# Maxima over partitions by TensorE and VectorE in place of GpSimd, in an attention and feed-forward kernel

## The chip, the cores and the metric

The kernel runs on one core of one Trainium2 chip. The core has five engines with a queue each: TensorE (PE in the profile: matmuls, with a part PEld for the loads of weights), VectorE (DVE), ScalarE (ACT), GpSimd (POOL) and SyncE (SP), which here issues DMAs. Each takes its instructions in order and waits at semaphores for the others. The metric is device time in microseconds (us) of one launch, less is better. Between runs of one kernel some 0.2% lie.

## The reference

A kernelised linear attention, followed by a feed-forward layer without a residual. For each of 8 batches and 8 heads, with 576 positions of 64 numbers:

```python
def phi(x):                                   # x is q or k, scaled by D ** -0.25
    proj = np.einsum('bhsd,md->bhsm', x, omega)          # 128 features
    h = proj - np.sum(x * x, axis=-1, keepdims=True) / 2.0
    h = h - np.max(h, axis=-1, keepdims=True)
    return np.exp(h) / np.sqrt(m)
q_p, k_p = (phi(q_s), phi(k_s))
kv = np.einsum('bhsm,bhsd->bhmd', k_p, v)
z = np.sum(k_p, axis=2)
num = np.einsum('bhsm,bhmd->bhsd', q_p, kv)
den = np.einsum('bhsm,bhm->bhs', q_p, z)[..., None] + 1e-06
x = num / den                                 # then (4608 tokens, 512)
h = x @ w_in                                  # 2048 wide
sp = np.where(h > 20.0, h, np.log1p(np.exp(np.minimum(h, 20.0))))
out = (h * np.tanh(sp)) @ w_out
```

All inputs and outputs are float32.

## The kernel before

**Numbers in two halves.** Most products run in float16, each float32 operand being split into a high half and the rest of it (`cast` and `rest`, lines 71 to 87), and a product of two such operands is three matmuls: low by high, high by low, high by high. For that the operands are brought into float16's range by a power of two: one scale per batch for `v` (tiles `p_v`, `s_v`), one for `w_in` and one for `w_out` (`p_w`, `s_w`). Each scale is the power of two below the largest magnitude in the whole operand: a maximum along the free dimension on VectorE, then a maximum over the 128 partitions, then the exponent's bits alone (`bitwise_and` with 0x7F800000), a floor, a reciprocal and a factor. `over_partitions` (L116) is the step over partitions: one GpSimd instruction, PARTITION_ALL_REDUCE (L118), which leaves the maximum in every partition. `pow2` (L131) is the whole sequence behind it.

**The stages.** Tokens go in 36 tiles of 128 (`q_task`), batches in 4 pairs of heads each (`k_task`), and the feed-forward layer in 18 chunks of 256 tokens. For each pair of heads: features of `k` (matmuls `pk`, L364), their maximum (`mxk`, L389) and difference (`ek`, L398) on VectorE, the exponential on ScalarE (L404), the halves `kp`, and the product with `v` into `pkv` (L485), where `vb` holds the halves of `v`: ScalarE applies the scale in place (L474), VectorE casts (L76), GpSimd subtracts (L83), for one part of the tasks. For each token tile: features `pq`, the same steps to `qn`, a transposing DMA to `qp` (L521), the product with `kv` into `pn` (L535), the division (L546 to L551), the halves `xs` and a transposing DMA to `xT`. For each chunk: `ff_in` with matmuls `ph` (L733), the activation on ScalarE (`mish`, L918), the halves `g` (L85), and `ff_out` with matmuls `po` (L1060). The last three chunks use sums and differences of blocks (`ff_in7`, `ff_out7`; `p_s`, `p_a`, `q_s`, `q_a`) in place of the whole products. The first chunk and the first two batches run in float32.

**GpSimd's part.** Besides the all-reduces it makes the low halves of `q` and `k` (`sq`, `sk`), of most `x` (`xs`) and of `v` (`vb`), all by L83.

**The order.** The program is written down in slots. `agenda` holds generators, each with the slot at which it goes on; `step()` runs those that are due and advances by one slot; a `yield n` inside a task means: go on n slots later. In the long middle part one slot comes with each group of 24 `ph` matmuls or of 12 `po` matmuls. `give()` starts the next `k_task` or `q_task`; when a batch's last `k_task` starts, `v_task` of the next batch is put 16 slots later (`V1`). At build time a scheduler orders each engine's queue: an instruction that is ready goes in the order in which it was written, and `tc.high_priority(PRIO)` moves what is inside it 400 places to the front. From the order follow all semaphores.

**`v_task` (L277).** It loads the batch's four `vf` tiles (a pool of 5 buffers, freed when the halves `vb` are made), takes a maximum of each on VectorE (`vmx`, L287), and then, at high priority, the maximum of the four (`vam`, L294) and `pow2`. `w_scale` (L204) does the same for a weight; `scale_w` (L1195) calls it at high priority. PSUM tiles with the tag "a" (`pk`, `pq`, `pn`, `pkv`, the transposed tiles) share 4 buffers. `idle` (L95) is a 128x512 float16 constant that the matmuls of `spin` read at the start.

Of the kernel before, what the change touches and what calls it, by code (L numbers as in the profile page):

```python
# [10 lines left out]
F32 = mybir.dt.float32  # L11
I32 = mybir.dt.int32
# [3 lines left out]
ALU = mybir.AluOpType  # L16
AX = mybir.AxisListType
# [5 lines left out]
TOP = 2.0 ** 14  # L23
KVC = 2.0 ** -23
TX = 2.0 ** 12
# [5 lines left out]
def tile_kernel(  # L31
# [10 lines left out]
    nc = tc.nc  # L42
    P = 128
# [17 lines left out]
    const = ctx.enter_context(tc.tile_pool(name="const", bufs=1))  # L61
# [3 lines left out]
    ps_a = ctx.enter_context(tc.tile_pool(name="ps_a", bufs=4, space=PSUM))  # L65
# [3 lines left out]
    act, dve, pool = nc.scalar, nc.vector, nc.gpsimd  # L69
# [25 lines left out]
    idle = const.tile([P, 512], F16, name="idle")  # L95
# [9 lines left out]
    ident = const.tile([P, P], F32, name="ident")  # L105
# [10 lines left out]
    def over_partitions(src, tag):  # L116
        allm = const.tile([P, 1], F32, name=f"allm_{tag}")
        pool.partition_all_reduce(  # L118
            out_ap=allm, in_ap=src, channels=P, reduce_op=bass.bass_isa.ReduceOp.max
        )  # L120
        return allm

    def top_over(p, tag, top):

        dve.tensor_scalar_max(p, p, 2.0 ** -100)
        s = const.tile([P, 1], F32, name=f"s_{tag}")
        dve.reciprocal(out=s, in_=p)
        dve.tensor_scalar_mul(s, s, top)
        return p, s

    def pow2(amax, tag, top):  # L131


        allm = over_partitions(amax, tag)
        p = const.tile([P, 1], F32, name=f"p_{tag}")
        dve.tensor_scalar(
            out=p.bitcast(I32), in0=allm.bitcast(I32), scalar1=0x7F800000, scalar2=None,
            op0=ALU.bitwise_and,
        )
        return top_over(p, tag, top)  # L140
# [27 lines left out]
    @contextmanager  # L168
    def behind(nth, first=0):
        with ExitStack() as st:  # L170
            for ins in anchors.get(nth, ())[first:]:
                st.enter_context(tc.issue_after(ins))
            yield
# [30 lines left out]
    def w_scale(n, tag):  # L204

        am = const.tile([P, 1], F32, name=f"am_{tag}")
        for i in range(NB):
            must(1, "w", n, i)
        dve.tensor_reduce(out=am, in_=wmax[n], axis=AX.X, op=ALU.max)
        return pow2(am, tag, TX)  # L210

    def w_split(n, i, s):
        src = flat32(slots[w_at(n, i)])
# [22 lines left out]
    def must(n, *key):  # L236
        assert done.get(key, 0) >= n, key
# [34 lines left out]
    def fetch_v(b, hp):  # L272
        t = sb.tile([P, 10, D1], F32, tag="vf", name=f"vf{b}_{hp}", bufs=5)
        nc.sync.dma_start(out=t, in_=vL[b, hp])
        return t

    def v_task(b):  # L277
        vt = []
        for hp in range(HP):
            vt.append(loaded.pop(f"v{b}_{hp}", None) or fetch_v(b, hp))  # L280
        if b == 0:
            vstate[0] = (vt, None, None)
        yield 3 if b else 6
        mx = sb.tile([P, HP], F32, tag="vmx", name=f"vmx{b}", bufs=2)
        for hp in range(HP):
            with behind(AV if b == 0 else None, 1):
                dve.tensor_reduce(  # L287
                    out=mx[:, hp:hp + 1], in_=vt[hp][:, :, 0:D], axis=AX.XY, op=ALU.max,
                    apply_absolute_value=True,
                )  # L290
            yield 0 if hp % 2 == 0 or b == 0 else 1
        am = sb.tile([P, 1], F32, tag="vam", name=f"vam{b}")
        with tc.high_priority(PRIO):
            dve.tensor_reduce(out=am, in_=mx, axis=AX.X, op=ALU.max)  # L294
            p, s = pow2(am, f"v{b}", TOP)
        vstate[b] = (vt, p, s)

    kv = {}
# [803 lines left out]
    W_LOAD, W_GAP, PRIO = 1, 1, 400  # L1102
# [76 lines left out]
    def give():  # L1179
        if given[0] < len(items):  # L1180
            it = items[given[0]]
            given[0] += 1
            start((k_task if it[0] == "k" else q_task)(given[0] - 1, *it[1:]))
            if it[0] == "k" and it[2] == HP - 1 and it[1] + 1 < B:
                start(v_task(it[1] + 1), V1)
# [9 lines left out]
    def scale_w(n):  # L1195
        with tc.high_priority(PRIO):
            p_w[n], s_w[n] = w_scale(n, f"w{n}")
# [4 lines left out]
    for what in PREL.split():  # L1202
# [8 lines left out]
        else:  # L1211
            loaded[f"w0_{i}"] = fetch_w(0, i, nc.sync)
    start(v_task(0), V0)
    for i, when in enumerate(FIRST):
        at(when, give)
# [93 lines left out]
```

## Time and profile before

| what | us |
|---|---|
| median of 3 runs | 952.98 (951.78 to 953.53) |
| the profiled execution, its own time | 954.62 |
| its span, first to last instruction | 952.8 |
| PE busy | 922.3 |
| DVE busy | 710.1 |
| ACT busy | 658.7 |
| POOL busy | 222.2 |
| mean granted clock of TensorE | 0.989 |

The ten all-reduces are short in the view by line: 3.7 us for the eight of `v`, 0.7 us for the two of the weights. They start at 27.37 (batch 0), 58.25 (w_in), 63.33 (batch 1), 110.55 (batch 2), 111.94 (w_out), 223.07, 296.73, 407.02, 518.61 and 638.89 us (batches 3 to 7). GpSimd's first elementwise work (L83) starts at 120.23 us.

How to read it: a row of a timeline has the start in us from the span's start, the busy time in us, engine, line, operation, the tile written and the tiles read, shapes, and the number of instructions merged into it; brackets at its end give the idle time of that engine just before it, and what ended it. A row of the waits has who waited for whom, the us in total, how often, and the longest. In the view by windows a row has the stretch, the busy time of PE, PEld, DVE, ACT and POOL with their instructions, the granted clock, the share of the DMA engines and GB/s. In groups by line the numbers behind the count are busy us, mean ns of one, and the idle time before them.

### The profile page before, as it was taken

To read this page: it belongs to the slowest core of one execution; us is meant where nothing else is said; L and a number is where in the kernel's file an instruction comes from. 1 tells how busy PE (TensorE), PEld (TensorE's weight loads), DVE (VectorE), ACT (ScalarE), POOL (GpSimd) and SP (SyncE) were. 2 spreads that over 40 slices of the span, in tenths; PEclk is the share of its full clock that TensorE was granted. 3 is DMA by queue.
4 is the path that set the end of the run, shared out by engine and by line. 5 is a ranking of instruction groups with operands and counts; after the bars stand their busy time and mean duration, and the time that the engine had idled before them with its cause. 6 is when DMAs were issued, how large, how long until landed. Compare 5 with 4: busy or idle time off the path is not lost. (4 is left out here: it accounts for less than half of the span.)

```text
span 952.8 us, 21094 instructions
## 1 busy us (share of the span) xinstructions
PE 922.3 (97%) x8774; PEld 689.1 (72%) x8774; DVE 710.1 (75%) x1226; ACT 658.7 (69%) x873; POOL 222.2 (23%) x141
## 2 busy tenths in 40 slices
PE   9799989999999999998999899999999999999998
PEld 6688764676677677776777667777777776779997
DVE  4799887686678778787687886776877766658775
ACT  5668975678777787867676866678876876345442
POOL 0000041343323323323221323224322222200000
PEclk9799999999999999999999999999999999999999
DMA  9766233421731356323532246321543137973421
GB/s 297 265 222 212 96 80 85 92 82 46 145 80 51 105 117 135 83 70 96 115 85 77 76 119 120 101 70 46 129 103 97 34 79 153 218 212 100 154 70 45
DMA packets 153056, 108.69 MB, mean 114 GB/s; under 512 B 112832, under 2 KB 125248, under 8 KB 152960
## 3 DMA queue, kind: packets, MB, share of 16 engines
q1 hardware_dynamic: 152640, 106.75, 43.0%
q8 instruction: 69, 1.13, 0.5%
q10 hardware_dynamic: 320, 0.59, 0.3%
q14 instruction: 27, 0.22, 0.1%
HBM read 63.14 MB, written 17.83 MB: 85 GB/s over the span
## 5 line engine op out<-in xcount | busy, mean ns | idle before, releaser
L733 PE MATMUL ph<-xT,w 128*128 128x256 f16 (+1 forms) x2816 | 345.6, 279 | 4.4 <-ACT h L918 4.4
L1060 PE MATMUL po<-wo,g 128*128 128x512 f16 x1344 | 308.6, 379 | 0.0
L733 PEld LDWEIGHTS <-w 128*128 128x128 f16 x2688 | 262.8, 98 | 54.2 <-issue 6.0
L1060 PEld LDWEIGHTS <-g 128*128 128x128 f16 x1344 | 127.2, 98 | 132.7
L918 ACT ACTIVATE h<-ph,us 128x512 f32<-128x512 f32 (+3 forms) x152 | 83.0, 572 | 49.3 <-PE ph L733 48.4
L85 DVE SCALAR_TENSOR_TENSOR g<-h,us,g 128x1024 f16<-128x1024 f32 (+3 forms) x76 | 103.3, 1371 | 14.6 <-ACT g L74 14.4
L83 POOL TENSOR_TENSOR sq<-fq,sq 64x1024 f16<-64x1024 f32 x31 | 72.7, 2347 | 145.5 <-issue 86.3
L83 POOL TENSOR_TENSOR sk<-fk,sk 64x1152 f16<-64x1152 f32 x24 | 59.3, 2471 | 113.7 <-ACT sk L74 92.2
L83 POOL TENSOR_TENSOR xs<-x,xs 128x512 f16<-128x512 f32 (+1 forms) x35 | 42.2, 1206 | 158.9 <-DVE xs L76 108.2
L918 ACT ACT_TABLE_LOAD x56 | 71.8, 1283 | 1.0
L404 ACT ACT_TABLE_LOAD x53 | 68.0, 1283 | 4.2 <-DVE ek L398 3.3
L83 DVE TENSOR_TENSOR qn<-eq,qn 128x1024 f16<-128x1024 f32 x31 | 39.1, 1260 | 33.2 <-ACT qn L74 33.2
L869 PEld LDWEIGHTS <-w 128*128 128x128 f16 x1008 | 59.0, 98 | 2.8
L404 ACT ACTIVATE eq<-eq,lnt 128x1024 f32<-128x1024 f32 x31 | 35.6, 1149 | 36.6 <-DVE eq L398 36.4
L389 DVE TENSOR_REDUCE mxq<-pq 128x4 f32<-128x512 f32 x72 | 46.7, 680 | 16.2 <-PE pq L364 15.3
L74 ACT ACTIVATE g<-h,us 128x1024 f16<-128x1024 f32 (+3 forms) x64 | 58.2, 933 | 0.9
L389 DVE TENSOR_REDUCE mxk<-pk 128x4 f32<-128x512 f32 (+1 forms) x96 | 49.5, 547 | 11.7 <-PE pk L379 4.3
L83 DVE TENSOR_TENSOR kp<-ek,kp 128x1152 f16<-128x1152 f32 x24 | 36.7, 1529 | 22.6 <-ACT kp L74 21.8
L83 POOL TENSOR_TENSOR vb<-vf,vb 128x640 f16<-128x640 f32 x24 | 39.0, 1627 | 61.7 <-DVE vb L76 43.9
L1007 PEld LDWEIGHTS <-gb 128*128 128x128 f16 x504 | 48.3, 98 | 5.2
L404 ACT ACTIVATE ek<-ek,lnt 128x1152 f32<-128x1152 f32 x24 | 30.1, 1256 | 30.0 <-DVE ek L398 29.9
L918 ACT ACTIVATE h<-h,us 128x1024 f32<-128x1024 f32 (+2 forms) x16 | 14.7, 931 | 48.1 <-DVE h L878 48.1
(165 smaller groups left out, 1363.3 us busy)
## 6 DMA issues: line engine op xcount, KB each, us to landing
w<-ds SPq DMA_DIRECT2D x48, 256.0 KB, 3.4
vf<-in_vL_dram SPq DMA_DIRECT2D x32, 325.0 KB, 3.1
out_dram<-o SPq DMA_DIRECT2D x36, 256.0 KB, 2.3
fq<-in_qT_dram SPq DMA_DIRECT2D x31, 256.0 KB, 3.5
fk<-in_kT_dram SPq DMA_DIRECT2D x24, 256.0 KB, 3.7
raw<-in_w_out_dram SPq DMA_DIRECT2D x5, 1024.0 KB, 8.1
wo<-in_w_in_dram SPq DMA_DIRECT2D x4, 1024.0 KB, 10.6
raw<-in_w_in_dram SPq DMA_DIRECT2D x4, 1024.0 KB, 15.0
```

The source lines that it names most:

```text
L74: act.activation(out, in_, AF.Copy, scale=scale)
L83: eng.tensor_tensor(out=out, in0=in_, in1=hi, op=ALU.subtract)
L85: eng.scalar_tensor_tensor(out=out, in0=in_, scalar=scale, in1=hi, op0=ALU.mult, op1=ALU.subtract)
L389: sub = dve.tensor_reduce(out=mx[:, lo:hi], in_=pp[:, :m, :], axis=AX.X, op=ALU.max, negate=by_act)
L404: last = act.activation(e, e, AF.Exp, bias=lnt)
L733: nc.tensor.matmul(out=ph[:, i, :], lhsT=wi(a, k, f) if c else wi0(k, f), rhs=xT[c][:, y, k, :] if c else xT0()[:, k, :], start=n == 0, st ...
L869: nc.tensor.matmul(out=ph[:, i, :], lhsT=left(gr, op_l, i, a, k), rhs=x_region(c, r)[:, y, k0 + k, :], start=n == 0, stop=n == len(mm) - 1,)
L918: act.activation(h[:, :, lo:hi], ph[:, :, lo:hi], AF.Mish, scale=us[:, 0:1])
L1007: nc.tensor.matmul(out=ps, lhsT=gT[c, n][:, i, a, f, :], rhs=rhs, start=f == 0 and (a, y) == (1, 0), stop=f == FG - 1 and (a, y) == (0, 0),)
L1060: nc.tensor.matmul(out=po[i], lhsT=gT[c, gr][:, a, f % FG, i * P:(i + 1) * P], rhs=wo(y, f), start=f == 0 and (a, y) == parts[0], stop=f = ...
```

## The change

From batch 2 on, and for `w_out`, the maximum over partitions is made by `pow2_pe`. TensorE transposes the 128x1 column into one row of a PSUM tile (`row`, tag "a"), VectorE takes the maximum of that row into one element and masks its exponent, and TensorE multiplies a row of 128 ones by that element, so that it stands in all partitions of a second PSUM tile (`every`, tag "a"). The rest on VectorE is as it was. The ones are written once, into the first partition of `idle`. Batches 0 and 1, and `w_in`, stay as they were.

In `v_task`, for those batches, the maximum `vam` and what follows have no high priority any more, and there are two places at which the task pauses for a slot: after `vam`, and between VectorE's masking and the product. For `w_out` the generator is run through at once, inside the high priority of `scale_w`.

```diff
+    ones = []
+
+    def pow2_pe(amax, tag, top):
+
+        row = ps_a.tile([P, P], F32, tag="a", name=f"row_{tag}")
+        nc.tensor.transpose(out=row[0:1, :], in_=amax, identity=ident)
+        one = const.tile([P, 1], F32, name=f"one_{tag}")[0:1]
+        dve.tensor_reduce(out=one, in_=row[0:1, :], axis=AX.X, op=ALU.max)
+        dve.tensor_scalar(
+            out=one.bitcast(I32), in0=one.bitcast(I32), scalar1=0x7F800000, scalar2=None,
+            op0=ALU.bitwise_and,
+        )
+        yield 1
+        if not ones:
+            ones.append(idle.bitcast(F32)[0:1, 0:P])
+            dve.memset(ones[0], 1.0)
+        every = ps_a.tile([P, 1], F32, tag="a", name=f"every_{tag}")
+        nc.tensor.matmul(out=every, lhsT=ones[0], rhs=one, start=True, stop=True)
+        p = const.tile([P, 1], F32, name=f"p_{tag}")
+        dve.tensor_scalar_max(p, every, 2.0 ** -100)
+        s = const.tile([P, 1], F32, name=f"s_{tag}")
+        dve.reciprocal(out=s, in_=p)
+        dve.tensor_scalar_mul(s, s, top)
+        return p, s
+
     def pow2(amax, tag, top):
...
         dve.tensor_reduce(out=am, in_=wmax[n], axis=AX.X, op=ALU.max)
-        return pow2(am, tag, TX)
+        if n == 0:
+            return pow2(am, tag, TX)
+        gen = pow2_pe(am, tag, TX)
+        while True:
+            try:
+                next(gen)
+            except StopIteration as stop:
+                return stop.value
...
         am = sb.tile([P, 1], F32, tag="vam", name=f"vam{b}")
-        with tc.high_priority(PRIO):
+        if b < 2:
+            with tc.high_priority(PRIO):
+                dve.tensor_reduce(out=am, in_=mx, axis=AX.X, op=ALU.max)
+                p, s = pow2(am, f"v{b}", TOP)
+        else:
             dve.tensor_reduce(out=am, in_=mx, axis=AX.X, op=ALU.max)
-            p, s = pow2(am, f"v{b}", TOP)
+            yield 1
+            p, s = yield from pow2_pe(am, f"v{b}", TOP)
         vstate[b] = (vt, p, s)
```

## The prediction, made before the changed kernel was run

> **What bounds the kernel now.** The page first: TensorE (PE) is busy for nearly the whole span, and what it does is a fixed amount of matmuls. So time can only be won where PE stands still or runs at a lower clock, and lost where it gets more to do or a new wait.
>
> ```profile
> span 952.8 us, 21094 instructions
> PE 922.3 (97%) x8774; PEld 689.1 (72%) x8774; DVE 710.1 (75%) x1226; ACT 658.7 (69%) x873; POOL 222.2 (23%) x141
> 520.00:560.00 40.00, 36.25 (x315) 25.34 (x313) 34.28 (x52) 27.45 (x33) 12.39 (x6) 0.96 0.26 76
> ```
>
> The third row is one stretch of the view by windows, with PE busy for 36.25 of 40 us and a granted clock of 0.96. Next come PE's own waits, and then its timeline after the start-up phase, of which I keep the rows that stand behind idle time (the brackets say how long and for whom).
>
> ```profile
> PE pn L535 <- DMA qp<-qn: 8.0, 7, 2.3
> PE pkv L485 <- DVE kp L83: 5.1, 2, 3.7
> 135.71 4.45 PE L733 MATMUL ph<-xT,w 128*128 128x256 f16 x24 [2.93 <-ACT h L918]
> 145.40 0.92 PE L535 MATMUL pn<-kv,qp 128*128 128x65 f16 x24 [1.80 <-DMA qp<-qn]
> 239.84 0.92 PE L535 MATMUL pn<-kv,qp 128*128 128x65 f16 x24 [2.31 <-DMA qp<-qn]
> 324.27 1.13 PE L485 MATMUL pkv<-vb,kp 128*128 128x65 f16 x30 [1.38 <-DVE kp L83]
> 448.27 2.78 PE L733 MATMUL ph<-xT,w 128*128 128x256 f16 x24 [1.49 <-ACT h L918]
> 452.64 0.92 PE L535 MATMUL pn<-kv,qp 128*128 128x65 f16 x24 [1.59 <-DMA qp<-qn]
> 544.65 1.13 PE L485 MATMUL pkv<-vb,kp 128*128 128x65 f16 x30 [3.75 <-DVE kp L83]
> 545.62 4.45 PE L733 MATMUL ph<-xT,w 128*128 128x256 f16 x24
> 562.41 0.96 PE L535 MATMUL pn<-kv,qp 128*64 128x65 f16 x48 [1.02 <-DMA qp<-qn]
> ```
>
> Eight gaps make 16.3 us; everywhere else PE runs on without a break. Two of them cost more than their length: the same 24 matmuls take 2.78 us at 448 and 4.45 us at 135 and at 545, right behind the two longest gaps, so 1.67 us more each, at a lowered clock. What precedes the gaps is an all-reduce on GpSimd (POOL). Around that of batch 6:
>
> ```profile
> 515.12 1.04 ACT L74 ACTIVATE sq<-fq 64x1024 f16<-64x1024 f32 x1
> 518.61 0.38 POOL L118 PARTITION_ALL_REDUCE allm_v<-vam  x1 [6.85 <-issue]
> 519.02 0.15 DVE L136 TENSOR_SCALAR p_v<-allm_v 128x1 int32<-128x1 int32 x1 [3.37 <-POOL allm_v L118]
> 526.14 2.90 POOL L83 TENSOR_TENSOR sq<-fq,sq 64x1024 f16<-64x1024 f32 x1 [7.15 <-DVE s L769]
> 529.12 1.73 POOL L83 TENSOR_TENSOR vb<-vf,vb 128x640 f16<-128x640 f32 x1
> 530.88 0.34 SPq L274 DMA_DIRECT2D vf<-in_vL_dram  x1
> 533.71 0.82 DVE L287 TENSOR_REDUCE vmx<-vf 128x1 f32<-128x640 f32 x1 [2.31 <-DMA vf<-in_vL_dram]
> L118 POOLq MODIFY_POOL_CONFIG  x12: 4/11/22, 2.2 to 633.1; - x12
> L83 POOLq MODIFY_POOL_CONFIG  x12: 83/83/83, 112.2 to 639.3; - x12
> ```
>
> The reduction itself is 0.38 us. But POOL does nothing for 6.85 us before it and 7.15 us after it, though the subtraction `sq` behind it had its input from ScalarE (ACT) at 516.16. The last two rows, of the view by line, name the reason: POOL's queue switches its program (MODIFY_POOL_CONFIG) when it goes from elementwise work (L83) to the reduction (L118), and again on the way back. So one reduction closes POOL for 14.4 us, and VectorE (DVE), whose next instruction reads the result, stands for 3.37 us. Behind it `vb` is late, so its `vf` buffer is freed late, the next `vf` load is issued late (530.88, 0.03 us after `vb` ends), and DVE waits again at `vmx`, 2.31 us. DVE's whole queue, `kp` in it, is behind by then, and the gap of 3.75 us at 544.65 waits for `kp`.
>
> **What the change removes.** Seven reductions leave POOL: batches 2 to 7 and w_out. Those of w_in and of batches 0 and 1 are issued before POOL's first elementwise work, so after the change POOL switches once and never again. I follow the gaps one by one. At 544.65: the chain just shown; 3.75 us and the 1.67 us of lowered clock go, 5.42. At 324.27 and 239.84:
>
> ```profile
> 308.26 1.74 POOL L83 TENSOR_TENSOR vb<-vf,vb 128x640 f16<-128x640 f32 x1
> 310.03 0.33 SPq L274 DMA_DIRECT2D vf<-in_vL_dram  x1
> 313.44 0.82 DVE L287 TENSOR_REDUCE vmx<-vf 128x1 f32<-128x640 f32 x1 [2.89 <-DMA vf<-in_vL_dram]
> 231.06 1.23 DVE L83 TENSOR_TENSOR qn<-eq,qn 128x1024 f16<-128x1024 f32 x1 [0.65 <-ACT qn L74]
> 231.18 3.10 POOL L83 TENSOR_TENSOR sq<-fq,sq 64x1024 f16<-64x1024 f32 x1 [7.73 <-DVE kv L85]
> 234.30 0.57 SPq L314 DMA_DIRECT2D fk<-in_kT_dram  x1
> 234.96 3.12 SPq L521 DMA_TRANSPOSE qp<-qn  x1
> ```
>
> The same chain with 2.89 us of DVE in it (gap 1.38). At 239.84 it goes through SyncE's queue: `qn` is ready at 232.29, but its transposition stands behind a load `fk`, whose buffer POOL's late `sq` frees at 234.28; 2.7 us are lost there, more than the gap of 2.31. At 145.40 the release is another, but of the same kind:
>
> ```profile
> 120.23 4.21 POOL L83 TENSOR_TENSOR sq<-fq,sq 64x1024 f16<-64x1024 f32 x2 [7.94 <-issue]
> 139.09 0.82 DVE L287 TENSOR_REDUCE vmx<-vf 128x1 f32<-128x640 f32 x1 [2.37 <-DMA vf<-in_vL_dram]
> ```
>
> POOL's first `sq` no longer waits 7.94 us, and the scale of batch 2 comes later (below), so that `vmx` of batch 3, whose 2.37 us hold up `qn` directly behind it, moves out of this place: 1.80 us. Together 5.42 + 1.38 + 2.31 + 1.80 = 10.9 us, which I can follow in rows. The gaps at 448, 452 and 562 (4.10 us) wait for queues behind a DVE that lags since a reduction, which I can't follow link by link: I take half, 2.05. The gap at 135 with its clock (2.93 + 1.67) waits for ACT; I take nothing, and keep the 4.6 for the range. Gain: 12.95 us.
>
> **What it adds.** Per reduction a transposition of a 128x1 column, a maximum over one row on DVE, and a product of a row of ones with one element. The trace has neither PE operation in this shape. The nearest rows:
>
> ```profile
> 117.71 0.49 PE L628 MATMUL pt<-ident,eq 128*128 128x128 f32 x3
> 118.13 0.69 PE L639 MATMUL pn<-kvf,qp 128*64 128x65 f32 x16
> L628 PE MATMUL pt<-ident,eq 128*128 128x128 f32 x40 | 8.8, 342 | 0.5 <-ACT eq L394 0.5
> ```
>
> From below 0.11 + 0.04 = 0.15 us for the pair (pace in a sequence: (0.49-0.27)/2, taking 0.27 as one's length, and 0.69/16), from above 0.34 + 0.34 = 0.68 (each alone, the product taken as a transposition). I take 0.4, between them, since they stand alone among other shapes: 7 x 0.4 = 2.8 us, bounds 1.1 and 4.8. On DVE one reduction more each, near the 0.15 us of the `p_v` row, and one fill with ones: 1 to 2 us in all beside 243 us of idle DVE, hidden; without that cover it would count with DVE's lag below.
>
> The waits are the greater question. PE is in order, so behind a waiting transposition or product stands everything. The transposition waits for `vam` (and for a PSUM buffer of tag "a"). For the batches it loses the priority that the reduction has now, so PE meets it at its place in the program. The program of before numbers its instructions as they are written down; the number of batch 6's reduction falls among PE matmuls that run at 578 to 583 us, those of batches 3, 4, 5 and 7 near 255, 355, 470 and 695, that of batch 2 near 145. `vam` of batch 6 is done by 516, so the transposition doesn't wait for it. The scale comes some 60 us later than now (`p_v` at 519.02); first used for `pkv` of batch 6, the 17th of the 24 `pkv` groups, it has 40 us left:
>
> ```profile
> 625.67 1.12 PE L485 MATMUL pkv<-vb,kp 128*128 128x65 f16 x30
> 430.86 1.06 PE L364 MATMUL pq<-om,sq 128*128 128x128 f16 x16
> 440.94 1.27 DVE L389 TENSOR_REDUCE mxq<-pq 128x4 f32<-128x512 f32 x2
> 580.58 1.06 PE L364 MATMUL pq<-om,sq 128*128 128x128 f16 x16
> 581.23 1.29 DVE L389 TENSOR_REDUCE mxq<-pq 128x4 f32<-128x512 f32 x2 [2.86 <-PE pq L364]
> ```
>
> The product waits for DVE's maximum. It stands one slot behind, some 2.7 us of PE work. Whether that is enough is DVE's lag: at 440.94 DVE takes a `pq` that PE had finished 9 us before, at 581.23 it stands idle for one. Lags like the first follow the reductions; at the new places DVE has caught up. So most of these waits should be nothing. For safety I give each of the 14 (two per reduction) what a `kp` or `qp` wait costs on average: (5.1 + 8.0) us over 24 `pkv` and 31 `pn` groups, 0.24 us: 3.4 us. From below 0; from above 2.55 us (5.1/2, a `kp` wait when it happens) once per reduction, 17.9. w_out keeps its priority and is worked out in one go, near 112 us, where PE is most likely to wait, for one DVE instruction or so.
>
> DVE in its turn waits for the transposition and for the product, with its own queue behind it; that takes the place of the 3.37 us for POOL, and is bounded by them (7 x 3.37 of idle time that DVE has).
>
> Sum: 12.95 - 2.8 - 3.4 = 6.8 us less. The profiled execution took 954.6 us (1.8 around its span) and would take 947.8; the median of the runs shown is 1.6 below it, so 952.98 - 6.8 = **946.2**.
>
> **The rivals.** (a) All gaps go, that at 135 too, and only 0.5 us per reduction is added: 10.9 + 4.1 + 4.6 - 3.5 = 16.1 less, 936.9. For it: all lie in DVE's and ACT's lag. Against it: a stall that goes uncovers the next one. (b) That happens to half of the gain: 6.5 - 6.2, 952.7. For it: gaps of several kinds, two of them behind ACT. (c) **Slower**: PE waits at the product. If DVE is a slot and more behind at the new places, as at 440.94, each of the seven costs 2.55 us: 17.9 + 2.8 - 12.95 = 7.8 more, 960.8. It decides from a mean of (12.95 - 2.8)/7 = 1.45 us per reduction. Against it stands the lag at 581.23. (d) The change doesn't do what it says: POOL's idle time around the reductions is not theirs, and nothing is won: 952.98 + 6.2 = 959.2. Against it the 7.15 us with the input ready. [...]
>
> **How the numbers follow.** Forecast (941 to 951) 0.54, (a) 0.13, (b) 0.15, (c) 0.12, (d) 0.06. What a measurement can tell from no change is about 0.2%, 1.9 us. Faster: 0.54 + 0.13 = 0.67; within: 0.15; slower: 0.18. The range goes from 938.5, which leaves out somewhat over half of (a), to 955.5, which leaves out most of (c) and (d): 0.2 in all.
>
> **What would show it.** Right: no POOL idle time of 7 us with its input there and no MODIFY_POOL_CONFIG after the first 70 us; no `vmx` wait of over 2 us after 300; the rows at 239, 324 and 544 without brackets, the clock at 1.0 from 520 to 560; the products released without a wait. Wrong: brackets at the new PE rows with DVE as the releaser, or new ones at `pk`, `pq` (the PSUM buffers that the two new tiles take), or gaps of the old kind at other places.

## The result, and the profile after

The changed kernel takes **940.12 us** (median of 4 runs, 939.40 to 940.96), the kernel before beside it 953.25 (4 runs, 951.78 to 953.66): ratio 0.9865, 95% interval 0.9848 to 0.9882, so 13.1 us less. The forecast was 946.2 with a range from 938.5 to 955.5. The direction was right and so was the chain behind the largest gap; the gain came out at nearly twice the size (13.1 us for 6.8). The profiled execution took 939.57 us.

The page's first lines, and one row of the view by windows (PE, PEld, DVE, ACT, POOL busy, then the granted clock), for the stretch in which PE had stood still for 3.75 us:

```profile
span 937.8 us, 21111 instructions
PE 920.5 (98%) x8795; PEld 689.4 (74%) x8795; DVE 707.1 (75%) x1234; ACT 658.9 (70%) x873; POOL 213.6 (23%) x134
520.00:560.00 40.00, 40.00 (x395) 28.89 (x393) 28.13 (x45) 32.32 (x36) 12.11 (x5) 1.00 0.41 90
```

PE's busy time is nearly that of before (920.5 and 922.3). What went is standing still: the stretch from 520 to 560 is full, at the full clock. The timeline of PE after the start-up phase, its rows behind idle time (two for DVE, at 182 and 828 us, of 0.29 and 0.57 us, are left out):

```profile
118.71 0.38 PE L148 MATMUL every_w<-one_w,idle 1*128 1x1 f32 x2 [0.81 <-DVE one_w L139]
...
139.88 0.92 PE L572 MATMUL pn<-kv,qp 128*128 128x65 f16 x24 [1.87 <-DMA qp<-qn]
...
156.42 0.92 PE L572 MATMUL pn<-kv,qp 128*128 128x65 f16 x24 [0.30 <-DMA qp<-qn]
...
381.33 0.55 PE L572 MATMUL pn<-kv,qp 128*128 128x65 f16 x12 [0.26 <-DVE ek L435]
...
790.36 0.92 PE L572 MATMUL pn<-kv,qp 128*128 128x65 f16 x24 [0.52 <-DMA qp<-qn]
```

Of the eight gaps of before, seven have no successor; one is left near 140. From 190 to 790 us PE waits once, for 0.26 us. Why shows in the view by line and, around the maximum of batch 6, in the timelines of POOL, SP, ACT and DVE:

```profile
L118 POOLq MODIFY_POOL_CONFIG  x2: 4/4/4, 2.2 to 2.2; - x2
L83 POOLq MODIFY_POOL_CONFIG  x2: 83/83/83, 62.3 to 62.4; - x2
```

```profile
506.27 0.16 DVE L330 TENSOR_REDUCE vam<-vmx 128x1 f32<-128x4 f32 x1
511.45 1.41 POOL L83 TENSOR_TENSOR vb<-vf,vb 128x640 f16<-128x640 f32 x1 [2.23 <-DVE vb L76]
512.89 0.33 SPq L306 DMA_DIRECT2D vf<-in_vL_dram  x1
515.80 0.82 DVE L319 TENSOR_REDUCE vmx<-vf 128x1 f32<-128x640 f32 x1 [0.40 <-DMA vf<-in_vL_dram]
519.54 1.04 ACT L74 ACTIVATE sq<-fq 64x1024 f16<-64x1024 f32 x1
520.71 2.12 POOL L83 TENSOR_TENSOR sq<-fq,sq 64x1024 f16<-64x1024 f32 x1 [7.85 <-issue]
```

POOL's program is switched for the last time at 62 us (the last switch was at 639). `vb` runs when DVE has made its half, the `vf` load follows it at once, and `vmx` finds its data after 0.40 us. The last row shows how to read idle time: POOL stands 7.85 us before this `sq`, as it did before the change, and the row names no releaser. But its input from ACT ends at 520.58, so here POOL is waiting for work; before, the input had been there for 10 us. It is nearly the same at every `sq` and `sk` after 100 us: where POOL was free, none starts more than 0.14 us behind its input, but for one `sk` (0.41 us, at 567.75).

The new PE work by tile (shortest, median, longest in ns, first and last start). A product is two instructions (two passes), which overlap and take 0.38 us together, as the row at 118.71 shows:

```profile
L136 PE MATMUL row_v<-ident,vam x6: 272/273/273, 140.6 to 679.8; 128*1 128x128 f32 x6
L148 PE MATMUL every_v<-one_v,idle x12: 245/256/267, 141.8 to 683.6; 1*128 1x1 f32 x12
```

No `row_v` and no `every_v` stands behind idle time; only `every_w` waits, 0.81 us.

How the two executions drift apart, from the start of the same `ph` matmul in both traces:

| before, us | after, us | difference | between this row and the one above |
|---|---|---|---|
| 46.9 | 45.6 | -1.3 | the load at the start; -0.7 to +0.2 in the runs below |
| 126.5 | 126.6 | 0.0 | w_out's pair and its wait: +1.3 |
| 171.9 | 167.7 | -4.2 | gaps at 135 and 145, pair of batch 2 |
| 244.1 | 237.3 | -6.7 | gap at 239 |
| 267.3 | 261.1 | -6.2 | pair of batch 3: +0.5 |
| 336.5 | 328.8 | -7.8 | gap at 324 |
| 473.3 | 463.6 | -9.7 | two pairs: +1.0; gaps at 448 and 452 |
| 567.6 | 551.3 | -16.4 | gaps at 544 (with its clock) and 562 |
| 590.9 | 575.0 | -15.8 | pair of batch 6: +0.5 |
| 952.8 | 937.8 | -15.0 | pair of batch 7; two short waits after 790 us |

So 1.3 of the 15.0 us between the two profiled executions come from the start, which the change doesn't touch; the other 13.7 are near the 13.1 between the medians.

### The profile page after: what moved, and what is told of

Read it like the earlier page. It is cut to its first block, busy times and chain, and to the rows that moved or that the text cites. A ratio compares the mean times of both kernels' runs of the same rounds, so it can differ in the third digit from the quotient of the medians.

```text
span 937.8 us, 21111 instructions
## 1 busy us (share of the span) xinstructions
PE 920.5 (98%) x8795; PEld 689.4 (74%) x8795; DVE 707.1 (75%) x1234; ACT 658.9 (70%) x873; POOL 213.6 (23%) x134
## 3 DMA queue, kind: packets, MB, share of 16 engines
q8 instruction: 69, 1.13, 0.5%
## 5 line engine op out<-in xcount | busy, mean ns | idle before, releaser
L83 POOL TENSOR_TENSOR sq<-fq,sq 64x1024 f16<-64x1024 f32 x31 | 70.5, 2275 | 253.6 <-ACT sq L74 177.8
L85 DVE SCALAR_TENSOR_TENSOR g<-h,us,g 128x1024 f16<-128x1024 f32 (+3 forms) x76 | 99.9, 1325 | 15.2 <-ACT g L74 14.9
L83 DVE TENSOR_TENSOR kp<-ek,kp 128x1152 f16<-128x1152 f32 x24 | 32.8, 1366 | 27.0 <-ACT kp L74 26.2
```

What stands on the lines that cost most here:

```text
L83: eng.tensor_tensor(out=out, in0=in_, in1=hi, op=ALU.subtract)
L85: eng.scalar_tensor_tensor(out=out, in0=in_, scalar=scale, in1=hi, op0=ALU.mult, op1=ALU.subtract)
```

## The experiments

Each ratio is to the kernel before, run beside it on the same chip; 0.001 is 0.95 us. On these chips the runs of one kernel lie up to 0.7% apart (953.25 to 960.32 us), more than the 0.2% told above, so a ratio counts with its interval. Two questions were open: is it GpSimd's closure, the place and priority of the work, or the reader's wait that the late gaps came from; and why did the early gaps near 135 go?

**The place alone.** The reductions go back to GpSimd, that of w_out too (`n in (0, 1)` for `n == 0`); batches 2 to 7 keep the new, unhurried place:

```diff
-            yield 1
-            p, s = yield from pow2_pe(am, f"v{b}", TOP)
+            yield 2
+            p, s = pow2(am, f"v{b}", TOP)
```

> All reductions on GpSimd again, but those of batches 2 to 7 without priority and as late as in the changed kernel (vam, two slots' pause, then the sequence). Theory A (GpSimd's program switch before and after each reduction makes the PE gaps): the switches stay, two per reduction, so most of the gaps come back, if at other places: 947 to 955 us. Rival B (what helps is that the v work of a batch lies later, where VectorE has caught up): 938 to 943 us. Rival C (it is VectorE's own wait for GpSimd, 7.4 us in all): between, as far as that wait is gone, about 946.

Measured: 953.15 us, ratio 0.9993 (0.9978 to 1.0008). All eight gaps are there (that near 239 with 0.72 us in place of 2.31), for example:

```profile
516.48 0.38 POOL L118 PARTITION_ALL_REDUCE allm_v<-vam  x1 [6.72 <-issue]
542.63 1.83 PE L522 MATMUL pkv<-vb,kp 128*128 128x65 f16 x30 [3.71 <-DVE kp L83]
```

Taking the priority away did not move the reduction: it still runs at 516 us. So this run doesn't test a later place on GpSimd; it shows that the edit to the place wins nothing without the change of engine.

**The engine alone.** TensorE's way, but at high priority and in one go (the generator is run through with the loop that w_out has; `...` stands for it):

```diff
-            dve.tensor_reduce(out=am, in_=mx, axis=AX.X, op=ALU.max)
-            yield 1
-            p, s = yield from pow2_pe(am, f"v{b}", TOP)
+            with tc.high_priority(PRIO):
+                dve.tensor_reduce(out=am, in_=mx, axis=AX.X, op=ALU.max)
+                gen = pow2_pe(am, f"v{b}", TOP)
...
```

> TensorE and VectorE make the maxima, but at the old place: high priority, in one go. Theory A: GpSimd stays in one program, so the gain stays but for what PE now waits at the product: 939 to 946 us. Rival B (the later place is what helps): 949 to 955 us. If PE waits a whole VectorE instruction at each of six products (about 1.3 us): 940 + 8 = 948.

Measured: 946.70 us, 0.9925 (0.9909 to 0.9941). The late gaps of before all go. But this edit, too, hardly moved the late work: the transposition of batch 6 starts at 564.79 us, in the changed kernel at 564.21, while GpSimd's reduction ran at 518.61. Only batch 2's moved, to 125.8 from 140.6. So the old place with the new engine was not tested for the late batches. What is lost against the changed kernel shows in PE's timeline:

```profile
128.36 0.38 PE L148 MATMUL every_v<-one_v,idle 1*128 1x1 f32 x2 [1.33 <-DVE one_v L139]
387.46 0.55 PE L578 MATMUL pn<-kv,qp 128*128 128x65 f16 x12 [2.64 <-DVE ek L441]
564.79 0.28 PE L136 MATMUL row_v<-ident,vam 128*1 128x128 f32 x1
836.60 1.50 PE L912 MATMUL p_s<-xT,w 128*128 128x128 f16 x24 [2.22 <-DVE h L921]
```

A product of batch 2 waits, at 387 a `pn` waits 2.64 us for `ek`, and at 836 a `p_s` waits 2.22 us (0.57 in the changed kernel). The new order of the queues costs some 6 us here, though only one product more shows a wait; which of its parts, the priority or the missing pauses, was not tested.

**GpSimd's closure alone.** The changed kernel, and for batches 3 to 7 the old reduction besides, into a spare tile that nobody reads:

```diff
             dve.tensor_reduce(out=am, in_=mx, axis=AX.X, op=ALU.max)
+            if b > 2:
+                with tc.high_priority(PRIO):
+                    pool.partition_all_reduce(out_ap=warm, in_ap=am, ...)
             yield 1
```

> The changed kernel, and beside it, for batches 3 to 7, the old reduction on GpSimd at its old priority, written to a tile that nobody reads. Theory A: five pairs of switches close GpSimd for 14 us each again, nobody waits for their result, and the gaps at 237, 317, 435 to 440 and 531 us come back for the most part: 946 to 954 us. Rival C (VectorE's wait for the result): nothing waits, so 939 to 942 us. Rival B (place): 939 to 942 us.

Measured: 948.90 us, 0.9958 (0.9943 to 0.9973): 0.0093 above the changed kernel, so 8.9 us of the 13 come back, with no engine waiting for the result. The scale of these batches still comes late (batch 6's transposition at 576.2 us), so the later place by itself doesn't keep the gaps away. View by line, then timelines:

```profile
L83 POOLq MODIFY_POOL_CONFIG  x12: 82/83/83, 63.3 to 635.4; - x12
```

```profile
513.49 1.10 POOL L333 PARTITION_ALL_REDUCE warm<-vam  x1 [6.50 <-DVE mxk L431]
521.79 2.12 POOL L83 TENSOR_TENSOR sq<-fq,sq 64x1024 f16<-64x1024 f32 x1 [7.20 <-DVE s L83]
523.99 1.41 POOL L83 TENSOR_TENSOR vb<-vf,vb 128x640 f16<-128x640 f32 x1
529.80 0.82 DVE L319 TENSOR_REDUCE vmx<-vf 128x1 f32<-128x640 f32 x1 [8.23 <-DMA vf<-in_vL_dram]
540.99 1.83 PE L527 MATMUL pkv<-vb,kp 128*128 128x65 f16 x30 [4.59 <-DVE kp L83]
```

This is the chain of the prediction, link by link: the program is switched (6.50 us of idle time), one short reduction, switched back (7.20), `vb` late, the `vf` load late, `vmx` stands 8.23 us on DVE, `kp` behind it, and PE stands 4.59 us, with the lowered clock (0.56 from 541 to 546 us; 1.83 us for what takes 1.13). Of the other late gaps, those near 239, 324 and 452 come back (1.14, 0.67 and 1.63 us, at 235, 319 and 446); those at 448 and 562 don't, so that these two hang on the closure is not shown.

**The reader's wait.** The same, and one DVE instruction at high priority that reads the spare tile:

```diff
+                    dve.tensor_scalar(
+                        out=warm.bitcast(I32), in0=warm.bitcast(I32), scalar1=0x7F800000,
+                        scalar2=None, op0=ALU.bitwise_and)
```

> As the kernel with the unread reduction, but VectorE has one instruction that reads its result, at the same priority as before, so that it stands for GpSimd at batches 3 to 7 as it did (7.1 us there in the trace of before). If that wait counts by itself: from 948.9 up to 951 or 952 us, near the whole gain of the late batches (944.4 + 7). If GpSimd's closure is all of it: 948.9 within a us.

Measured: 0.9975 (0.9955 to 0.9995). The wait is there,

```profile
DVE warm L336 <- POOL warm L333: 6.9, 4, 3.3
```

6.9 us of DVE in four waits, but the ratio is only 0.0017 (1.6 us) above the run without a reader, and the intervals overlap. A cost of the reader is not shown; by the intervals it is at most some 4 us, and the closure is the main part.

**The late batches alone.** Batch 2 and w_out on GpSimd, batches 3 to 7 by TensorE (`b < 3` for `b < 2`, and `n in (0, 1)` for `n == 0`):

> Batches 3 to 7 by TensorE, batch 2 and w_out by GpSimd as before. Theory A, from the steps of the two traces (2.5 + 1.6 + 2.9 + 6.7 us at the later gaps, 5 pairs of 0.52 us to pay): 953.2 - 13.7 + 2.6 = 942 us, with the gap at 135 us there again. If the gain is made at the start (batch 2 and w_out): 949 us.

Measured: 944.38 us, 0.9900 (0.9884 to 0.9917). No gap from 190 to 793 us. At the start:

```profile
134.48 2.78 PE L770 MATMUL ph<-xT,w 128*128 128x256 f16 x24 [2.36 <-ACT h L955]
143.91 1.42 PE L572 MATMUL pn<-kv,qp 128*128 128x65 f16 x24 [3.21 <-DMA qp<-qn]
```

So by the ratios the change has a late part of some 9.5 us and an early part of some 3.3 (0.9900 to 0.9865).

**The early part: w_out alone back on GpSimd** (`n in (0, 1)` for `n == 0`):

> The changed kernel with w_out's maximum by GpSimd again (one switch back at 112 us); batches 2 to 7 by TensorE. If the gap at 135 us was GpSimd's late first sq: the gap is there again, 943 to 945 us. If it was batch 2's v work on ScalarE and VectorE between 122 and 139 us, which now lies later: no gap, and the product's wait of 0.8 us for w_out saved, 939 to 940 us.

Measured: 0.9891 (0.9844 to 0.9937). The interval is wide and takes in the changed kernel's 0.9865, but in the trace the early gain is gone:

```profile
134.07 2.78 PE L770 MATMUL ph<-xT,w 128*128 128x256 f16 x24 [2.15 <-ACT h L955]
162.17 0.92 PE L572 MATMUL pn<-kv,qp 128*128 128x65 f16 x24 [3.35 <-DMA qp<-qn]
```

That looks like the closure at 112 us (7.65 us of POOL's idle time behind that reduction). The next run contradicts it.

**A shorter product, and w_out's product a slot later.** The masked maximum is a power of two, so its upper half is an exact bfloat16, and the product is one pass in place of two (one instruction of 0.17 us, in place of two that take 0.38 together). `scale_w`'s generator for w_out pauses for its slot and leaves the high priority before the product:

```diff
-            ones.append(idle.bitcast(F32)[0:1, 0:P])
+            ones.append(idle.bitcast(BF16)[0:1, 0:P])
-        nc.tensor.matmul(out=every, lhsT=ones[0], rhs=one, start=True, stop=True)
+        nc.tensor.matmul(out=every, lhsT=ones[0], rhs=one.bitcast(BF16)[:, 1:2], ...)
...
-    at(slot[0] + W_LOAD + W_GAP + 2, scale_w, 1)
+    start(scale_w_out(), W_LOAD + W_GAP + 2)
```

> The changed kernel with the product in bfloat16 (one pass; a power of two is exact in it) and, for w_out, a slot's pause between the transposition and the product, which has no priority. Seven products shorter by about 0.2 us, and the wait of w_out's product (0.8 us of PE, 1.6 of the weight load) gone: 937.5 to 939.5 us. If the pause makes w_out's halves late: 941 us or more.

Measured: 0.9859 (0.9834 to 0.9883), no better than the changed kernel. A pair now costs 0.32 us of drift in place of 0.52. But the early gap is back, although GpSimd is open:

```profile
133.54 2.78 PE L765 MATMUL ph<-xT,w 128*128 128x256 f16 x24 [1.86 <-ACT h L950]
```

In the changed kernel ACT's queue holds one activation `h` ahead of the exponential `eq` and its two table loads; in the kernel before, that `h` and, on DVE, `qn` come later (first three rows, then those of the changed kernel):

```profile
132.51 1.15 ACT L404 ACTIVATE eq<-eq,lnt 128x1024 f32<-128x1024 f32 x1
134.97 0.69 ACT L918 ACTIVATE h<-ph,us 128x512 f32<-128x512 f32 x1
139.83 1.22 DVE L83 TENSOR_TENSOR qn<-eq,qn 128x1024 f16<-128x1024 f32 x1
...
124.83 8.02 PE L770 MATMUL ph<-xT,w 128*128 128x256 f16 x72
...
128.20 0.67 ACT L955 ACTIVATE h<-ph,us 128x512 f32<-128x512 f32 x1
128.88 1.28 ACT L441 ACT_TABLE_LOAD   x1
130.18 1.15 ACT L441 ACTIVATE eq<-eq,lnt 128x1024 f32<-128x1024 f32 x1
131.35 1.28 ACT L955 ACT_TABLE_LOAD   x1
...
134.31 1.23 DVE L83 TENSOR_TENSOR qn<-eq,qn 128x1024 f16<-128x1024 f32 x1 [0.40 <-ACT qn L74]
```

In the changed kernel PE then runs three groups of `ph` in one go. Before, and in the last two runs, that `h` stands behind the exponential and the table loads (1.28 + 1.15 + 1.28 us), and PE waits for ACT. Nothing in the change names this order; the scheduler of the build writes it.

**That order alone.** The kernel before, with the sixth call of `mish` moved ahead:

```diff
-    def mish(sp, h, ph):
+    def mish(sp, h, ph, n=[], ahead=ExitStack()):
+        n.append(1) or len(n) == 6 and ahead.enter_context(tc.high_priority(40))
         for us, lo, hi in sp:
             act.activation(h[:, :, lo:hi], ph[:, :, lo:hi], AF.Mish, scale=us[:, 0:1])
+        ahead.close()
```

> The kernel before, all ten reductions on GpSimd, with one activation (the sixth of the function `mish`) issued ahead of ScalarE's first `eq` exponential and its two table loads, as it stands in the changed kernel. TensorE then has the three groups of 24 `ph` matmuls near 125 us in one go. If the early 4 us of the change hang on that order alone, the gap of 2.9 us near 135 goes, with the 1.67 us of lowered clock behind it, and 4 us go in all: ratio 0.9955. All later gaps stay, that of 3.7 us near 544 with its clock too. Rival: ScalarE, or the transfer of `qp`, is late because GpSimd was closed from 112 to 120 us; then as much reappears as a gap near 140 to 160 us, and the ratio is 0.998 to 1.000.

Measured: 957.90 us, 1.0030 (1.0013 to 1.0047), slower. The rival's gap appears, larger than it said:

```profile
129.59 0.81 ACT L474 ACTIVATE vf<-vf,s_v 128x640 f32<-128x640 f32 x1
130.31 0.67 ACT L918 ACTIVATE h<-ph,us 128x512 f32<-128x512 f32 x1
131.03 2.78 PE L733 MATMUL ph<-xT,w 128*128 128x256 f16 x24 [1.34 <-ACT h L918]
139.69 0.82 DVE L287 TENSOR_REDUCE vmx<-vf 128x1 f32<-128x640 f32 x1 [2.44 <-DMA vf<-in_vL_dram]
146.04 1.50 PE L535 MATMUL pn<-kv,qp 128*128 128x65 f16 x24 [6.22 <-DMA qp<-qn]
```

The edit did what it should, `h` now stands ahead of `eq`, but PE still waits 1.34 us for it: ACT has scaled `vf` of batch 2 three times by then (2.35 us in all), which in the changed kernel comes later. PE arrives at `pn` earlier, but `qn` still stands behind the `vmx` of batch 3, so all that was won is waited for there, and the 24 `pn` behind it take 1.50 us for 0.92, as at a lowered clock. The same edit on top of the run with the late batches alone:

> The run with batches 3 to 7 by TensorE, batch 2 and w_out by GpSimd (0.99 of the kernel before), with the same activation issued ahead. If the order is all, the two early reductions on GpSimd cost nothing, and with two pairs fewer on TensorE (1.0 us) and no wait at w_out (1.3 us) this is a little faster than the changed kernel: 0.985. Rival: GpSimd's closure at 112 us is behind the early gaps; then it stays at 0.989 to 0.990, with gaps near 140 to 160 us.

Measured: 0.9891 (0.9870 to 0.9912), no different from that run without the edit (0.9900), with the same gap of `pn` at 146 us.

So the rows speak for an early part that needs two things: ACT's order, and batch 2's work on `v` later, so that the scaling of `vf` is out of the way of `h`, and the `vmx` of batch 3 out of the way of `qn`. With the order alone the wait moves to 146; with batch 2's later scale but not the order (w_out back on GpSimd, and the shorter product with its later w_out) PE waits at 134 and again at 161 to 162, where the `vmx` of batch 3 stands just ahead of the next `qn`; in the changed kernel it stands behind it. The changed kernel has both, and keeps 1.87 us at 139.88. That these two are all is argued: no run has the order and the later scale of batch 2 with w_out on GpSimd.

**The price of a pair.** Transposition and product three times for batches 3 to 7:

```diff
-        nc.tensor.transpose(out=row[0:1, :], in_=amax, identity=ident)
+        times = 3 if tag in ("v3", "v4", "v5", "v6", "v7") else 1
+        for _ in range(times):
+            nc.tensor.transpose(out=row[0:1, :], in_=amax, identity=ident)
...
+        for _ in range(times):
+            nc.tensor.matmul(out=every, lhsT=ones[0], rhs=one, start=True, stop=True)
```

> The transposition and the product each three times in batches 3 to 7. If PE has no slack there, each further pair costs the 0.52 us by which the two traces drift apart at each pair: 5 x 2 x 0.52 = 5.2 us, 945.3 us. If the pairs lie in gaps: 940 us.

Measured: 0.9885 (0.9860 to 0.9909). In PE's timeline

```profile
252.68 0.49 PE L138 MATMUL row_v<-ident,vam 128*1 128x128 f32 x3
256.58 0.82 PE L151 MATMUL every_v<-one_v,idle 1*128 1x1 f32 x6
```

copies in a row overlap: three transpositions take 0.49 us, not 3 x 0.27. The drift grows by 1.18 us per batch in place of 0.52, so 0.66 us for two more pairs, 3.3 us in all, and the ratio's 0.0020 (1.9 us) agrees within its interval. A pair that is repeated is no measure of a pair that stands alone.

**The version that remains.** The shorter product alone, everything else as in the changed kernel (its two changed lines stand above, ahead of the `...`):

> The changed kernel with one difference: the product with ones runs in bfloat16 (the masked maximum is a power of two, so its upper half holds it exactly), one pass of 0.17 us in place of two passes of 0.38. The order of every engine is that of the changed kernel, so the early order of ScalarE's queue stays: no row behind idle time at 133 to 135 us, as the changed kernel has none. If a pair costs 0.32 us of TensorE in place of 0.52, seven of them save 1.4 us: 0.0015 of the ratio, so about 0.985 if the changed kernel beside it is again at 0.9865. Rival: the two passes lay in TensorE's path only in part, and the two come out alike. Second rival: the earlier 0.9859 was short because of the place of w_out's product; then the gap at 133 us comes back here as well, although the order is unchanged.

and the changed kernel beside it:

> The changed kernel itself once more, beside the run with the shorter product, so that a difference of 0.15% has a neighbour on the same chip: ratio 0.9865, within 0.0017 as its interval was; again no gap at 135 and one of 1.9 us near 140 to 145.

Measured: 938.79 us, 0.9845 (0.9831 to 0.9860), beside 939.48 us, 0.9854 (0.9837 to 0.9871). ACT's order stays in both, and with it the gap near 135 stays away:

```profile
141.18 0.92 PE L572 MATMUL pn<-kv,qp 128*128 128x65 f16 x24 [2.11 <-DMA qp<-qn]
256.08 0.17 PE L148 MATMUL every_v<-one_v,idle 1*128 1x1 bf16 x1
```

The product is 0.17 us in place of 0.38. Both kernels beat that of before; of the 0.7 us between them the intervals tell nothing, and the 1.4 us expected are neither shown nor excluded. In the profiled execution of the changed kernel beside it 1.5 us of the early gain are lost again behind the same gap, where the matmuls take longer, as at a lowered clock (rows in the last section).

## Why the prediction was right, and where its size was off

| step of the prediction | predicted, us | measured, us |
|---|---|---|
| gap at 544 with its clock | 5.42 less | gone |
| gaps at 324 and 239 | 3.69 less | gone |
| gaps at 135 (with its clock) and 145 | 1.80 of 6.40 less | 6.40 gone, but 1.87 at 139 |
| gaps at 448, 452 and 562 | 2.05 of 4.10 less | all gone |
| seven pairs on PE | 2.8 more | 7 x 0.52 = 3.6 more |
| fourteen waits of PE | 3.4 more | 0.81 more, at w_out |
| sum | 6.8 less | 19.6 - 1.9 - 3.6 - 0.8 = 13.3 less |

The medians differ by 13.1 us. PE's short waits that no row names make 1.6 us before and 1.9 us after; the prediction's "everywhere else PE runs on without a break" passed over those of before.

**The cause was right for the late gaps.** GpSimd's closure of 14 us per reduction (10 us of it, at batch 6, with work waiting) carries most of the late part: the closure alone, unread, brings 8.9 us back although the scale stays late. Whether the later place of the scale wins something besides is open, since neither run that was to change the place alone moved the late work.

**Sizes that were off.** First, the gaps at 448, 452 and 562, "which I can't follow link by link: I take half". They went whole. That added 2.05 us to the gain. DVE's lag after a reduction, to which the prediction put all three, is shown for the one at 452 alone, which the unread reduction brings back. Second, the fourteen waits, priced at the mean of `kp` and `qp` waits "For safety". The argument beside them, that DVE has caught up at the new places, was the better evidence: no `every_v` waits, and 2.6 of the 3.4 us fall away. Batch 2 in the run at high priority shows what a product earlier and without a pause costs: a wait of 1.33 us. Its later products, without a pause too, don't wait. Third, a pair costs 0.52 us, not 0.4, within the bounds of 0.15 and 0.68.

**A step that failed.** The gaps at 135 and 145. The reason given for 145 was right as far as it went: `vmx` of batch 3 moved out, and `qn` starts at 134.31 in place of 139.83. But the row that waits for `qp` did not go, since PE arrives there as much earlier. The gap at 135, counted as nothing, went instead, by an order of ACT's queue that the diff doesn't mention; the trace of before couldn't show it. Together they gave 4.5 us where 1.80 was put. That part of the gain is luck as far as the prediction goes; in another execution of the same kernel 1.5 us of it went again, to matmuls as long as at a lowered clock.

**The rivals.** (a), all gaps gone with 936.9, was nearest: gaps go as it says, but for 1.9 us. The 940.12 lie just below the prediction's own 941 to 951, on the side of (a), to which it gave 0.13. (c), PE waiting at the product, shows only at w_out. (d) falls with the unread reduction.

**The signs.** No long POOL idle time with the input there, no late switch of the program, the batches' products without a wait (w_out's waited 0.81 us), the clock at 1.0 from 520 to 560: as said. One sign failed:

```profile
584.66 0.82 DVE L319 TENSOR_REDUCE vmx<-vf 128x1 f32<-128x640 f32 x1 [4.25 <-DMA vf<-in_vL_dram]
```

A `vmx` waits 4.25 us after 300 us, and PE has no bracket near it. A wait of DVE need not reach PE.

## What to carry to other kernels

A short instruction that makes an engine change its program is priced by the closure around it (here 0.38 us of work in 14 us of closure): look at the idle time on both sides, ask whether the input was there, and test it with a copy that nobody reads. Where several gaps seem to trail one cause, put down both sums, with those that can't be followed and without them; half is a guess. A stop that goes can leave as long a one behind it on another engine, as at 146 here (6.22 us), and a few instructions' shift can reorder another engine's queue by several us (here an `h` of ACT from 134.97 to 128.20), so compare the queues of the two traces before the gain is put down to the edit. The same holds for an experiment: look in its trace whether the edit moved what it was to move.

## What the runs showed of the hardware

**The reduction over partitions.** Here the way over TensorE and VectorE is 0.52 us of PE per reduction, GpSimd's 0.38 us with 14 us of closure, and the kernel is 1.35% faster with the former. So in this kernel the way over TensorE and VectorE is the better one. POOL's idle time before the late reductions is 6.0 to 6.9 us, in the kernel before and in the two runs above that have them. It is there at each of the fourteen that the views show, and the way back to elementwise work costs as much again, 6.9 to 7.7 us.

**The clock.** The length of a gap alone doesn't decide whether the clock falls behind it. In the trace of before the granted clock is 0.62 from 135.7 to 140.2 us, where 24 `ph` matmuls take 4.45 us, and 1.00 from 448.0 to 451.1, where 24 take 2.78; in the rows below the clock is read from such lengths. Four runs, in this order: the place alone, the changed kernel beside the shorter product, w_out back on GpSimd, and the shorter product with w_out a slot later:

```profile
135.44 4.45 PE L770 MATMUL ph<-xT,w 128*128 128x256 f16 x24 [2.78 <-ACT h L955]
...
141.07 0.99 PE L572 MATMUL pn<-kv,qp 128*128 128x65 f16 x24 [1.89 <-DMA qp<-qn]
142.07 1.91 PE L401 MATMUL pq<-om,sq 128*128 128x128 f16 x16
...
165.87 3.32 PE L770 MATMUL ph<-xT,w 128*128 128x256 f16 x24
...
161.28 0.92 PE L567 MATMUL pn<-kv,qp 128*128 128x65 f16 x24 [3.20 <-DMA qp<-qn]
```

Behind 2.78 us of idle time 24 `ph` matmuls took 4.45 us in place of their usual 2.78. Behind 1.89 us 16 `pq` matmuls took 1.91 us in place of 1.06; in the first execution of that kernel the granted clock stayed at 1.00, from 139.8 to 144.0, behind 1.87 us, shown at 139.88. With w_out back on GpSimd the 24 `pn` behind 3.35 us (162.17, above) took their usual 0.92, but the 24 `ph` at 165.87 took 3.32 in place of 2.78. Behind 3.20 us at 161.28 the lengths stayed the usual ones: 0.92 for these `pn`, 2.78 for the 24 `ph` at 164.72. So three of the five gaps had longer matmuls behind them. What else decides stays open.
